# A dense–SiLU–dense forward and backward kernel: GpSimd clears the semaphores before its wait for the last store, waits in the barrier's release, and takes the last count off behind it

## The chip, the cores and the metric

The kernel runs on one core of one Trainium2 chip. The metric is the device's time for one execution in microseconds (us), on that core; lower is better. The "span" of a run is the part of it from the program's first instruction to the end of its last one. Every run told here was in the fast state (one-look runs are marked "unknown" for lack of a second run to compare), at a granted TensorE clock of 0.999 to 1.000, and every kernel gave the right result.

## The reference, cut to what matters

```
x: (1, 2048, 640)   w1: (640, 1536)   w2: (1536, 640)   grad_out: (1, 2048, 640)   all bf16
h   = silu(x @ w1)
out = h @ w2
returns out and the gradients of x, w1 and w2 for grad_out
```

The last output to be finished is the gradient of w1. Nothing of the mathematics is touched by the change. What matters is how the program ends.

## The kernel before: its end

The gradient of w1 is stored in pieces; the last piece is split into one of 384 and one of 128 columns, so that the very last store is small:

```python
# ... (inside the loop over the last block of w1's gradient)
for k, (lo, hi) in enumerate(((0, FC - P), (FC - P, FC))):
    gp = ps_h.tile([P, FC], FP32, name="hp")
    # ... 16 matmuls into gp[:, lo:hi]
    g1 = s1pool.tile([P, FC], dt_in, name="g1")
    # ... copied by ScalarE (k == 0) or VectorE (k == 1)
    store = nc.sync.dma_start(out=gw1_v[:, dt_, fc * FC + lo:fc * FC + hi], in_=g1[:, lo:hi])
    last_stores.append(store.ins.name)
last_stores_end_on_pool(nc, last_stores)
```

After that the framework appends a closing block: SyncE waits for everything that is still open, all engines meet in a first barrier, GpSimd clears the program's semaphores (here numbers 99 to 110), and all engines meet in a second barrier. In a barrier each of the four other engines raises a "gather" semaphore (96), GpSimd waits for four of these, then raises a "release" semaphore (97) by four, and each engine takes one off as its receipt. `last_stores_end_on_pool` edits this block when the program is finalized:

```python
def last_stores_end_on_pool(nc, names):
    def move(nc):
        # ... lanes: the semaphores of the two last stores; waits: SyncE's list of open waits
        late = [w for lane in reversed(lanes) for w in waits if w.id == lane]
        waits = [w for w in waits if w.id not in lanes]           # SyncE no longer waits for them
        # ...
        drain, gather, release, reset, clear, drain2, gather2, release2 = pool
        # ... gather2, reset, clear, drain2 are taken out
        reset = copy.replace(reset, sync_info=mybir.SyncInfo(on_wait=late, on_update=[]))
        for i in (drain2, clear, reset, gather2):                 # put back in the order
            end.insert(to, i)                                     # gather2, reset, clear, drain2

    nc.at_finalize(move)
```

So GpSimd's closing sequence before is: gather, release | gather2, wait for store 107, drain that waits for store 108 (`reset`), clear 99 to 110, drain, release2. Numbers 107 and 108 are the semaphores of the two last stores; a store has landed when its semaphore has got 16 more counts. After this the runtime's own closing code follows, which is no part of the program.

## Time and profile before

| kernel before | |
|---|---|
| time, first three runs | 320.31 us median (319.86 to 320.56) |
| span of the profiled run | 318.5 us |
| TensorE busy | 315.5 us, 99% |
| granted TensorE clock | 1.000 |
| last store: issue to its 16th count | 1.443 us |
| its 16th count to the end of the span | 0.423 us |
| end of the span to the last count of the runtime's barriers | 1.908 us |

The page of the profile of the kernel before: its span, busy time by engine (microseconds, share of the span, number of records), and the chain of work that ended last, by engine.

```profile
span 318.5 us, 3634 instructions
PE 315.5 (99%) x1529; PEld 147.5 (46%) x1529; DVE 103.0 (32%) x183; ACT 77.4 (24%) x139; POOL 0.7 (0%) x6
...
PE 98%; DMA 1%; DVE 0%; issue 0%; DVEq 0%; SPq 0%
```

TensorE is the bottleneck from 2.8 us to 316.2 us, and everything else hides behind it. A change that touches neither matmuls nor loads can act on the start or on the end alone.

The timeline of the kernel before from 311.5 us on (start, duration, engine, line, operation), its last lines. "SPq" is SyncE's queue: two issues, merged.

```profile
315.38 0.49 ACT L431 ACTIVATE g<-hp 128x384 bf16<-128x384 f32 x1 [5.46 <-PE hp L422]
315.89 1.08 SPq L434 DMA_DIRECT2D out_dram<-g  x2
316.32 0.29 DVE L433 CAST g<-hp 128x128 bf16<-128x128 f32 x1 [2.80 <-PE hp L422]
```

The timeline shows the engines' work and the DMA issues only, so nothing after 316.97 us is in it, though the span lasts to 318.51. The last 1.5 us are semaphore and drain instructions of the sequencers. The view of one source line counts them; here that of the line to which the closing block is put, GpSimd alone, from 310 us (count, durations in ns as minimum/median/maximum, first and last start):

```profile
L481 POOLq EVENT_SEMAPHORE  x5: 17/17/17, 317.4 to 318.4; - x5
L481 POOLq DRAIN  x2: 34/56/78, 318.1 to 318.3; - x2
L481 POOLq EVENT_SEMAPHORE_RANGE_CLEAR  x1: 96/96/96, 318.2 to 318.2; - x1
```

Both drains and the clear start at or after 318.1 us, behind the last store. The trace's own records have them one by one (start in us from the span's start, duration in ns, what; "16th count" is the last of the sixteen updates of a store's semaphore):

```
316.644  332  SyncE   issue of the last store (128x128)
317.512       16th count of semaphore 107 (the store before the last)
317.714   17  GpSimd  gather2
317.810   17  GpSimd  wait for 107
318.087       16th count of semaphore 108 (the last store)
318.111   78  GpSimd  drain, waits for 108
318.217   96  GpSimd  range clear 99..110
318.342   34  GpSimd  drain
318.406   17  GpSimd  release2
318.459   51  TensorE receipt; ends at 318.510, the end of the span
318.743, .777, .984, 319.028, .052, .150, .189, .223, .270    semaphore 2 (the runtime's barrier)
319.169 to 319.837   the runtime clears all semaphores
320.061 to 320.418   semaphore 2 again, nine times
```

Two things are needed to read this. The Trainium skill, "Perfetto Trace Analysis", section "Sequencer-only Instruction (DRAIN, etc)", says that a record begins when all awaited semaphores are satisfied, not when the wait begins. The trace agrees: the drain that waits for 108 has its start 24 ns after the 16th count, although GpSimd was free 0.28 us earlier. So the cost of a sequence has to be read from the spacing of starts, and the wait is the gap. And "Runtime: NRT & Kernel Launch", section "Semaphores 0–2 are reserved", names semaphore 2 as that of the runtime's barrier; its section "The ~15µs preamble/postamble breakdown" puts a barrier and a clearing of semaphores after the kernel. The records above agree, with the nine counts from 318.743 to 319.270. Below, each of these nine is called a step of the runtime's barrier; the third is at 318.984. That each step belongs to one engine is a reading.

### The profile page before, as it was taken

How to read it: one execution, taken by the hardware profiler on the slowest of the kernel's cores; microseconds unless marked ns; L12 is line 12 of the kernel's file. 1: busy time of each engine (PE TensorE's matmuls, PEld its weight loads, DVE VectorE, ACT ScalarE, POOL GpSimd, SP SyncE). 2: the span in 40 equal slices, each digit the busy share in tenths (PEclk: the TensorE clock that was granted, in tenths of full speed). 3: DMA queues.
4: the chain of work that ended last, by engine and by line, in shares of the span. 5: the costliest groups of instructions: out<-in, count | busy, mean ns of one | idle time of the engine just before them, and what ended most of it. 6: DMA issues, size and time to landing. Idle time of an engine off the chain costs nothing.

```text
span 318.5 us, 3634 instructions
## 1 busy us (share of the span) xinstructions
PE 315.5 (99%) x1529; PEld 147.5 (46%) x1529; DVE 103.0 (32%) x183; ACT 77.4 (24%) x139; POOL 0.7 (0%) x6
## 2 busy tenths in 40 slices
PE   9999999999999999999999999999999999999997
PEld 6644444444444444444444444444444444444444
DVE  1387641477410187710147741000000100001001
ACT  3492000644201354411064520110100001001010
POOL 0000000000000000000000000000000000000000
PEclk9999999999999999999999999999999999999999
DMA  9999999999799874492635079919999999996011
GB/s 242 332 182 190 238 283 239 350 291 311 233 229 320 199 228 113 145 302 83 166 105 145 0 259 268 216 24 299 254 243 261 251 209 341 245 264 217 33 35 49
DMA packets 147264, 66.85 MB, mean 210 GB/s; under 512 B 113328, under 2 KB 146736, under 8 KB 147248
## 3 DMA queue, kind: packets, MB, share of 16 engines
q1 hardware_dynamic: 146960, 66.33, 82.6%
q10 hardware_dynamic: 288, 0.30, 0.3%
q8 instruction: 12, 0.20, 0.2%
q14 instruction: 4, 0.03, 0.0%
HBM read 9.18 MB, written 28.97 MB: 120 GB/s over the span
## 4 chain that ended last, share of the span: by engine, by line
PE 98%; DMA 1%; DVE 0%; issue 0%; DVEq 0%; SPq 0%
PE hp L302 33%; PE hp L286 16%; PE hp L391 16%; PE hp L442 15%; PE hp L223 14%; PE hp L254 3%; PE hp L422 1%; DMA x_nat<-in_x_dram 1%; PE tp L212 1%; DVE g L433 0%; DVEq L433 0%; SPq L470 0%
## 5 line engine op out<-in xcount | busy, mean ns | idle before, releaser
L286 PE MATMUL hp<-goT,w2T 128*128 128x512 bf16 x240 | 56.9, 379 | 0.0
L302 PE MATMUL hp<-aT,w_nat 128*128 128x512 bf16 x240 | 52.5, 379 | 0.0
L302 PE MATMUL hp<-ghT,w1T 128*128 128x512 bf16 x240 | 52.5, 379 | 0.0
L391 PE MATMUL hp<-a_blk,go_nat 128*128 128x512 bf16 x240 | 52.0, 379 | 0.0
L442 PE MATMUL hp<-gh_blk,x_nat 128*128 128x512 bf16 x224 | 48.5, 379 | 0.0
L223 PE MATMUL hp<-xT,w_nat 128*128 128x512 bf16 x200 | 48.2, 379 | 0.0
L310 ACT ACTIVATE oT<-hp 128x512 bf16<-128x512 f32 x24 | 14.4, 598 | 104.3 <-PE hp L302 104.3
L232 ACT ACTIVATE aT<-hp 128x512 bf16<-128x512 f32 x48 | 28.5, 614 | 37.4 <-PE hp L223 30.4
L302 PEld LDWEIGHTS <-w1T 128*128 128x128 bf16 x240 | 23.5, 98 | 28.3
L302 PEld LDWEIGHTS <-w_nat 128*128 128x128 bf16 x240 | 23.5, 98 | 28.3 <-DMA w_nat<-in_w_dram 0.2
L391 PEld LDWEIGHTS <-go_nat 128*128 128x128 bf16 x240 | 23.5, 98 | 28.3
L286 PEld LDWEIGHTS <-w2T 128*128 128x128 bf16 x240 | 23.5, 98 | 28.3
L293 DVE SCALAR_TENSOR_TENSOR ghT<-ghT,hp 128x512 bf16<-128x512 bf16 x48 | 32.5, 682 | 7.0 <-PE hp L286 7.0
L442 PEld LDWEIGHTS <-x_nat 128*128 128x128 bf16 x224 | 21.9, 98 | 26.4
L312 DVE CAST oT<-hp 128x512 bf16<-128x512 f32 x16 | 11.0, 691 | 70.6 <-PE hp L302 70.6
L239 DVE SCALAR_TENSOR_TENSOR ghT<-aT,v 128x512 bf16<-128x512 bf16 x48 | 32.6, 686 | 0.3
L223 PEld LDWEIGHTS <-w_nat 128*128 128x128 bf16 x200 | 19.5, 98 | 23.4
L238 DVE TENSOR_SCALAR v<-t 128x512 bf16<-128x512 f32 x48 | 20.1, 425 | 28.1 <-ACT t L236 28.1
L236 ACT ACTIVATE t<-hp 128x512 f32<-128x512 f32 x44 | 26.5, 620 | 0.0
L453 DVE CAST g<-hp 128x512 bf16<-128x512 f32 x7 | 4.8, 692 | 47.0 <-PE hp L442 28.0
L401 DVE CAST g2T<-hp 128x512 bf16<-128x512 f32 x7 | 4.8, 692 | 46.1 <-PE hp L391 46.1
L399 ACT ACTIVATE g2T<-hp 128x512 bf16<-128x512 f32 x8 | 4.8, 597 | 47.0 <-PE hp L391 47.0
(24 smaller groups left out, 43.7 us busy)
## 6 DMA issues: line engine op xcount, KB each, us to landing
aT_scr<-aT SPq DMA_DIRECT2D x4, 1536.0 KB, 6.2
ghT_scr<-ghT SPq DMA_DIRECT2D x4, 1536.0 KB, 8.0
out_dram<-o_sb SPq DMA_DIRECT2D x8, 640.0 KB, 3.5
oT_scr<-oT SPq DMA_DIRECT2D x4, 640.0 KB, 4.3
go_nat<-in_grad_out_dram SPq DMA_DIRECT2D x4, 640.0 KB, 6.5
gxT_scr<-oT SPq DMA_DIRECT2D x4, 640.0 KB, 5.7
w_nat<-in_w_dram SPq DMA_DIRECT2D x1, 1920.0 KB, 12.5
x_nat<-in_x_dram SPq DMA_DIRECT2D x3, 640.0 KB, 7.0
```

The source lines that it names most:

```text
L223: nc.tensor.matmul(hp[:], lhsT=w1_nat[:, dt_, ft * P:(ft + 1) * P], rhs=xT[:, dt_, :], start=(dt_ == 0), stop=(dt_ == DT - 1),)
L232: nc.scalar.activation(aT[:, ft, :], hp[:], ACT.Silu)
L236: nc.scalar.activation(t[:], hp[:], ACT.Tanh, scale=0.5)
L238: nc.vector.tensor_scalar(out=v[:], in0=t[:], scalar1=-0.5, scalar2=0.5, op0=ALU.mult, op1=ALU.add)
L239: nc.vector.scalar_tensor_tensor(out=ghT[:, ft, :], in0=aT[:, ft, :], scalar=1.0, in1=v[:], op0=ALU.subtract, op1=ALU.mult)
L286: nc.tensor.matmul(gp[:], lhsT=w2T[:, dt_, ft * P:(ft + 1) * P], rhs=goT[:, dt_, :], start=(dt_ == 0), stop=(dt_ == DT - 1),)
L293: nc.vector.scalar_tensor_tensor(out=ghT[:, ft, :], in0=ghT[:, ft, :], scalar=1.0, in1=gp[:], op0=ALU.add, op1=ALU.mult)
L302: nc.tensor.matmul(op_[:], lhsT=w_all[:, ft, dt_ * P:(dt_ + 1) * P], rhs=rhs_all[:, ft, :], start=(ft == 0), stop=(ft == FT - 1),)
L310: nc.scalar.activation(oT[:, dt_, :], op_[:], ACT.Copy)
L312: nc.vector.tensor_copy(out=oT[:, dt_, :], in_=op_[:])
L391: nc.tensor.matmul(gp[:], lhsT=go_nat[:, st, dt_ * P:(dt_ + 1) * P], rhs=a_blk[:, st, :], start=(st == 0), stop=(st == ST - 1),)
L442: nc.tensor.matmul(gp[:], lhsT=x_nat[:, st, dt_ * P:(dt_ + 1) * P], rhs=gh_blk[:, st, :], start=(st == 0), stop=(st == ST - 1),)
```

## The change

The intent: 0.295 us of drains and clearing lie between the first instruction after the arrival of the last store (318.111) and the release (318.406). Do the clearing while the store is still in flight. The semaphore of the last store cannot be cleared then, so the cleared range is split around it, the release itself waits for the store, and one more instruction takes the 192 counts off afterwards.

```diff
@@ -52,21 +53,52 @@
         end = blocks[-1].instructions
         at = next(k for k, i in enumerate(end) if i.engine == mybir.EngineType.SP)
         waits = list(end[at].sync_info.on_wait)
-        late = [w for lane in reversed(lanes) for w in waits if w.id == lane]
+        late = [w for lane in lanes for w in waits if w.id == lane]
         assert len(late) == len(names) and not end[at].sync_info.on_update
         waits = [w for w in waits if w.id not in lanes]
         end[at] = copy.replace(end[at], sync_info=mybir.SyncInfo(on_wait=waits, on_update=[]))
+
         pool = [i for i in end if i.engine == mybir.EngineType.Pool]
         drain, gather, release, reset, clear, drain2, gather2, release2 = pool
         assert gather2.sync_info.on_wait and not release2.sync_info.on_wait
-        assert all(i.sync_info is None or not i.sync_info.on_wait for i in (reset, clear, drain2))
-        closing = {i.name for i in (reset, clear, drain2, gather2)}
+        assert all(i.sync_info is None for i in (reset, clear, drain2))
+        last = late[-1]
+        first, stop = reset.reset_range_start, reset.reset_range_stop
+        assert first <= last.id < stop and list(clear.instr[12:15]) == [1, first, stop - 1]
+        cleared = []
+        for lo, hi in ((first, last.id), (last.id + 1, stop)):
+            if lo < hi:
+                cleared.append(
+                    copy.replace(reset, name=nc.get_next_instruction_name(), reset_range_start=lo, reset_range_stop=hi)
+                )
+                cleared.append(
+                    copy.replace(
+                        clear,
+                        name=nc.get_next_instruction_name(),
+                        instr=clear.instr[:13] + (lo, hi - 1) + clear.instr[15:],
+                        ant_dict={**clear.ant_dict, "range_first": lo, "range_last": hi - 1},
+                    )
+                )
+        cleared[0] = copy.replace(cleared[0], sync_info=mybir.SyncInfo(on_wait=late[:-1], on_update=[]))
+        (total,) = gather2.sync_info.on_update
+        off = copy.replace(total, id=last.id, ant_name=last.ant_name, update_value=last.wait_value)
+        tail = [gather2, *cleared, drain2]
+        tail.append(
+            copy.replace(
+                release2, sync_info=mybir.SyncInfo(on_wait=[last], on_update=list(release2.sync_info.on_update))
+            )
+        )
+        tail.append(
+            copy.replace(
+                release2, name=nc.get_next_instruction_name(), sync_info=mybir.SyncInfo(on_wait=[], on_update=[off])
+            )
+        )
+        closing = {i.name for i in pool[3:]}
         to = next(k for k, i in enumerate(end) if i.name == reset.name)
         for k in reversed(range(len(end))):
             if end[k].name in closing:
                 del end[k]
-        reset = copy.replace(reset, sync_info=mybir.SyncInfo(on_wait=late, on_update=[]))
-        for i in (drain2, clear, reset, gather2):
+        for i in reversed(tail):
             end.insert(to, i)
 
     nc.at_finalize(move)
```

GpSimd's closing sequence after it: gather, release | gather2, drain that waits for 107, clear 99 to 107, drain, clear 109 to 110, drain, release2 that waits for 108, count-off of 108. No other engine's instructions differ.

## The prediction

> **What bounds the kernel now.** TensorE: the busy table gives PE 315.5 of 318.5 us (99%), the chain of waits PE 98%, at full granted clock (1.000). The change touches no matmul, transfer or buffer, only instructions after the last store is issued, so it can act on the last microsecond alone.
>
> **That microsecond, from the trace's records of sequencer instructions (us from the span's start).** SyncE issues the last store at 316.644. GpSimd collects the second barrier's arrivals at 317.714; its wait for the first of the two last stores starts at 317.810 and costs nothing (landed at 317.512). The last store's 16th count comes at 318.087. Only then GpSimd runs drain 318.111 (78 ns), range clear 318.217 (96 ns), drain 318.342 (34 ns), release 318.406. TensorE's receipt ends the span at 318.510. So 0.295 us (318.111 to 318.406) is serial between the store's arrival and the release: the most that the change can take off.
>
> **What the change does.** It moves that work ahead of the last wait, puts the wait on the release, and splits the clear in two (9 semaphores, then 2), each behind a drain. It adds a drain and a clear, drops a separate wait, and adds one instruction behind the release that subtracts the last count.
>
> **Costs.** By start-to-start spacing in the trace, a drain that doesn't wait takes 64 ns, one that waited 106, the 12-semaphore clear 125, a semaphore instruction 66 to 96. After 317.714 GpSimd starts its first drain at about 317.80, then 64 to 106 (drain), 120 (clear), 64 (drain), 105 (clear), 64 (drain): estimate of the release, 318.22 to 318.26. The store is there at 318.09. So the moved work, about 0.42 us, doesn't fit in the gap of 0.30 us before the store's arrival; the release becomes bound by GpSimd's own sequence, and the gain there is about 0.17 us (0.08 to 0.24), not 0.295.
>
> **What is given back.** The count-off stands after the release on GpSimd: +0.08 us (estimate from the 79 ns spacing of two of its semaphore instructions). The Trainium skill's page "Runtime: NRT & Kernel Launch", section "The ~15µs preamble/postamble breakdown", says that a barrier of all engines and a reset of the semaphores follow the kernel. The trace agrees: semaphore 2 is raised nine times from 318.743 to 319.270. Its third step comes 207 ns after its second, against 38 ns in the other barriers; I take the late third engine to be GpSimd (the order is a guess). If so, GpSimd ends the kernel's time and the 0.08 us is paid in full; if not, it is hidden.
>
> **Prediction.** The span falls by about 0.17 us (to 318.2 to 318.45), the time by about 0.1 us: 320.2 us. Runs of before spread from 319.86 to 320.56, so the range is 319.75 to 320.6. Faster by over 2%: 0.01; within 2%: 0.98; slower: 0.01.
>
> **What would show each step.** Right: matmul rows, clock and DMA unchanged; two clears on GpSimd between 317.8 and 318.25, at 105 to 125 ns each; the release over 0.05 us after the last store's 16th count; one more semaphore instruction 80 to 96 ns after it; the runtime barrier shifted earlier by less than the release. Wrong: the release within 30 ns of the 16th count (the clears fitted, gain near 0.3 us); or the barrier shifted as much as the release (count-off free).
>
> **What would make it wrong.** A last store that lands later than in this one profile and leaves the clears more room; a second drain or clear much dearer than the first; a barrier that waits for another engine than GpSimd; above all scatter between runs, larger than the effect.

## The result, and the profile after

| | before | after |
|---|---|---|
| time, median of 6 runs each | 320.16 us (319.55 to 320.56) | 320.07 us (319.55 to 320.62) |
| ratio after/before | | 1.000, 95% interval 0.9985 to 1.0016 |
| span of the profiled run | 318.51 us | 317.68 us |
| **from the issue of the last store:** | | |
| 16th count of the last store | +1.443 | +1.445 |
| release2 | +1.762 | +1.664 |
| GpSimd's last instruction starts | +1.762 | +1.742 |
| third step of the runtime's barrier | +2.340 | +2.320 |
| last count of the runtime's barriers | +3.774 | +3.755 |

A ratio is the mean time of one kernel's fast runs over that of the other's of the same rounds, so it isn't quite the ratio of the medians quoted. The time is the same to within its interval of 0.15%, some 0.5 us. All outputs are right.

The page of the kernel after, the same three lines:

```profile
span 317.7 us, 3608 instructions
PE 313.5 (99%) x1501; PEld 147.3 (46%) x1529; DVE 103.0 (32%) x183; ACT 77.4 (24%) x139; POOL 0.7 (0%) x6
...
PE 98%; DMA 1%; issue 1%; DVE 0%; DVEq 0%; SPq 0%
```

The span looks 0.83 us shorter, which would be a gain of 0.3%. It isn't one. (Nor has the kernel lost 28 matmuls: PE has 1501 records against 1529, but the weight loads are 1529 in both; a few matmul records are missing from this trace.) The chain that ended last shows where the span differs. Here are its pieces in the first 16 us (start, duration, what), of before:

```profile
0.08 2.73 DMA x_nat<-in_x_dram
...
2.85 1.78 PE tp L212 x15
4.64 9.39 PE hp L254 x80
```

and of after:

```profile
0.08 2.55 DMA x_nat<-in_x_dram
...
2.68 1.78 PE tp L244 x15
4.46 8.84 PE hp L286 x80
```

The first load of x landed 0.18 us sooner, and the first 80 matmuls, which begin while loads of w1 are still arriving, took 0.55 us less: 0.73 us in all, in code that the change doesn't touch. From the 43rd weight load (6.4 us) to the last (316.0 us) the two traces run in step, with an offset of 0.728 to 0.730 us in all but one of these 1487 loads. Only the remaining 0.098 us can belong to the change. It was the fastest of the six runs that was profiled: the spans of all six run from 317.7 to 318.8 us. Scatter of the start is what moves the time of this kernel from run to run, and it is several times the whole effect. So from here on landmarks are counted from the issue of the last store, where that scatter is gone.

GpSimd in the closing block of the kernel after, from 310 us (the same view of one source line; the block's line number has moved from 481 to 513):

```profile
L513 POOLq EVENT_SEMAPHORE  x5: 17/17/17, 316.6 to 317.7; - x5
L513 POOLq DRAIN  x3: 40/60/76, 317.1 to 317.5; - x3
L513 POOLq EVENT_SEMAPHORE_RANGE_CLEAR  x2: 45/68/92, 317.2 to 317.4; - x2
```

The two clears are there, of 92 and 45 ns, with a third drain. Record by record:

```
after the last store's issue, us (duration ns); spacing to the next start, ns
+1.095 (17)  gather2                    95
+1.190 (76)  drain, 107 has landed     105
+1.295 (92)  clear 99..107             121
+1.416 (60)  drain                      89
+1.445       16th count of the last store
+1.505 (45)  clear 109..110             75
+1.580 (40)  drain                      84
+1.664 (17)  release2, waits for 108    78
+1.742 (17)  count-off of 108
+1.768       TensorE's receipt ends, the end of the span
+2.001 +2.036 +2.320 +2.364 +2.387 ...  the runtime's barrier
```

When the store arrives, the second drain is still running. The release comes 0.219 us after the 16th count, where an instruction that was waiting for it would start about 0.02 us after. And of the 0.098 us that the release gained, the runtime's barrier kept 0.020: GpSimd's last instruction had moved by only 0.020 us, because of the count-off behind the release. From GpSimd's last instruction to the third step it is 0.578 us in both traces.

### The profile page after: what moved, and what is told of

Read it like the earlier page. It is cut to its first block, busy times and chain, and to the rows that moved or that the text cites. A ratio compares the mean times of both kernels' runs of the same rounds, so it can differ in the third digit from the quotient of the medians.

```text
span 317.7 us, 3608 instructions
## 1 busy us (share of the span) xinstructions
PE 313.5 (99%) x1501; PEld 147.3 (46%) x1529; DVE 103.0 (32%) x183; ACT 77.4 (24%) x139; POOL 0.7 (0%) x6
## 4 chain that ended last, share of the span: by engine, by line
PE 98%; DMA 1%; issue 1%; DVE 0%; DVEq 0%; SPq 0%
PE hp L334 32%; PE hp L318 16%; PE hp L423 16%; PE hp L474 15%; PE hp L255 13%; PE hp L286 3%; PE hp L454 1%; DMA x_nat<-in_x_dram 1%; PE tp L244 1%; DVE g L465 0%; DVEq L465 0%; SPq L502 0%
```

## The experiments

The theory: (a) the release is bound by GpSimd's own sequence of two clears and three drains and not by the store; (b) GpSimd is the third engine of the runtime's barrier and the last to arrive there, so everything behind the release on GpSimd is paid in full. The rivals: the small differences are scatter; the count-off is hidden because the runtime's barrier waits for another engine; the landing of the store bounds the end whoever waits for it.

All landmarks are from one profile of each kernel, in us after the issue of the last store. The last column is the time of that profiled run minus the moment of the issue in it; it follows the landmarks, which shows that the runtime's barriers are part of the measured time.

| kernel | release2 | GpSimd's last | 3rd step | last count | time minus issue |
|---|---|---|---|---|---|
| before | 1.762 | 1.762 | 2.340 | 3.774 | 3.65 |
| before_again | 1.764 | 1.764 | 2.342 | 3.775 | 3.64 |
| after | 1.664 | 1.742 | 2.320 | 3.755 | 3.64 |
| after_again | 1.633 | 1.711 | 2.290 | 3.720 | 3.60 |
| count_off_by_12 | 1.644 | 2.584 | 3.158 | 4.618 | 4.49 |
| count_off_by_12_on_sp | 1.634 | 1.634 | 2.207 | 3.863 | 3.74 |
| no_count_off | 1.638 | 1.638 | 2.217 | 3.674 | 3.55 |
| one_clear | 1.465 | 1.543 | 2.121 | 3.585 | 3.46 |
| no_clear | 1.463 | 1.541 | 2.119 | 3.551 | 3.42 |
| early_pool_waits | 1.554 | 1.632 | 2.205 | 3.637 | 3.51 |
| early_sp_waits | 1.440 | 1.440 | 2.013 | 3.446 | 3.31 |
| early_one_clear | 1.260 | 1.260 | 1.839 | 3.271 | 3.15 |

### Controls: the two kernels once more

No edit.

> The changed kernel once more, as a control for one profile's scatter. All landmarks are counted from the issue of the last store. In the first profiles: before has the last store's 16th count at +1.443, the release at +1.762, the third step of the runtime's barrier at +2.340 and its last count at +3.774 us; after has +1.445, +1.664, +2.320 and +3.755. My theory (the release is bound by GpSimd's own chain of two clears; the count-off behind it is paid in full): the same four landmarks within 0.03 us. Rival (the small differences between the two kernels are scatter of the landmarks): release and third step move by 0.05 us or more from the first profile of this kernel.

> The kernel before once more, as a control for the landmarks of one profile, counted from the issue of the last store. Theory: 16th count +1.44, release +1.76, third step of the runtime's barrier +2.34, each within 0.03 us, so that the changed kernel's two profiles (third step +2.32 and +2.29) are earlier by 0.02 to 0.05. Rival (the difference of the two kernels is scatter): third step at +2.31 or less.

Measured: after_again's release at +1.633 and third step at +2.290; before_again's release at +1.764 and third step at +2.342. In each profile of the changed kernel the time from gather2 to release2 is 0.569 us; the 0.031 us by which its two releases differ is that of gather2 (+1.095 and +1.064), which waits for TensorE's arrival at the second barrier. So the release gained 0.098 and 0.129 us over before, and the third step 0.020 and 0.050. after_again misses the 0.03 us that its expectation had allowed, by 0.001 us at the release and 0.005 us at the last count (+3.720 against +3.755), but stays short of the 0.05 us of its rival. The odd one is the first profile: in the nine profiles in which no clear stands ahead of it, gather2 comes at +1.064 to +1.076, but for the +1.095 there. One profile of a kernel repeats to about 0.03 us here. So the gain at the release is clear of the scatter; that at the third step is of the scatter's size, and its exact amount is not shown. The time: 320.14 us against 320.38 us of before, ratio 0.9999 (0.9984 to 1.0014), which can't resolve it.

### The count-off taken in twelve steps, on GpSimd

```diff
@@ -91,3 +91,6 @@
-        tail.append(
-            copy.replace(
-                release2, name=nc.get_next_instruction_name(), sync_info=mybir.SyncInfo(on_wait=[], on_update=[off])
+        part = copy.replace(off, update_value=16)
+        for _ in range(last.wait_value // 16):
+            tail.append(
+                copy.replace(
+                    release2, name=nc.get_next_instruction_name(), sync_info=mybir.SyncInfo(on_wait=[], on_update=[part])
+                )
@@ -95 +97,0 @@
-        )
```

> GpSimd takes the last store's count of 192 off in 12 steps of 16 instead of one. Theory (GpSimd is the last engine into the runtime's barrier, so each instruction behind its release is paid): third step of the barrier at about +3.18 us after the last store's issue, 11 times 0.078 = 0.86 us later than in the changed kernel, and the time 0.86 us longer (ratio to before near 1.0025). Rival (the runtime's barrier waits for another engine, the count-off is hidden): third step and time unchanged, or up by far less than 0.86 us.

Measured: third step at +3.158, the count-offs 78 ns apart, and 0.574 us from GpSimd's last instruction to the third step. The first and second steps stayed at +1.982 and +2.016: two other engines had arrived and waited for the third. The time was 321.11 us against 320.38 us, ratio 1.0031 (1.0015 to 1.0048). The extra instructions are paid in full; the third engine is GpSimd, and it is the one that the runtime waits for. The prediction's guess of the order is thereby shown for this step.

### The same twelve steps, on SyncE

```diff
@@ -91,5 +90,0 @@
-        tail.append(
-            copy.replace(
-                release2, name=nc.get_next_instruction_name(), sync_info=mybir.SyncInfo(on_wait=[], on_update=[off])
-            )
-        )
@@ -102,0 +98,11 @@
+        sp_last = [i for i in end if i.engine == mybir.EngineType.SP][-1]
+        at_sp = next(k for k, i in enumerate(end) if i.name == sp_last.name)
+        for _ in range(12):
+            end.insert(
+                at_sp + 1,
+                copy.replace(
+                    sp_last,
+                    name=nc.get_next_instruction_name(),
+                    sync_info=mybir.SyncInfo(on_wait=[], on_update=[copy.replace(off, update_value=16)]),
+                ),
+            )
```

> The same 12 steps of 16, but on SyncE, behind its receipt of the release; none on GpSimd. Theory: GpSimd's third step comes 0.078 us earlier than in the changed kernel (about +2.24 us after the last store's issue), and SyncE, which stands at the fifth step, has some 0.3 to 0.5 us of slack against 12 times about 0.067 = 0.80 us, so the barrier ends 0.2 to 0.5 us later than in the changed kernel, not 0.8. Rival (an instruction at the end costs the same on every engine): +0.7 to 0.8 us.

Measured: the third step at +2.207. SyncE's last instruction ended at +2.425 and the fifth step came at +2.554, so with twelve steps SyncE, the fifth engine, does become the last. The barriers ended at +3.863, 0.11 to 0.14 us later than in the changed kernel, where twelve steps on GpSimd had cost 0.86 to 0.90. My expectation of 0.2 to 0.5 us was too high: SyncE's count-offs are 57 to 74 ns apart, 60 in the mean, and not 67, and it needs only 0.129 us from its last instruction to its step. The plainest comparison is with the next run, which has no count-off at all and ends at +3.674: the twelve steps cost 0.189 us on SyncE and 0.944 us on GpSimd. The same work costs far less on an engine that isn't awaited. The time, 320.02 us against 320.38, ratio 0.9992 (0.9977 to 1.0008), can't resolve the 0.09 us by which the landmarks put it behind before.

### No count-off

```diff
@@ -91,5 +90,0 @@
-        tail.append(
-            copy.replace(
-                release2, name=nc.get_next_instruction_name(), sync_info=mybir.SyncInfo(on_wait=[], on_update=[off])
-            )
-        )
```

> The changed kernel without the count-off; the last store's semaphore is left at 192 for the runtime to clear. Theory: release unchanged (about +1.66 us after the last store's issue), third step of the barrier 0.078 us earlier (about +2.24), so the whole is 0.10 us shorter than before where the changed kernel was 0.02. Time minus span about 1.79 us as before, against 1.86 for the changed kernel. Rival (the count-off is hidden): third step stays at +2.32 us and time minus span at 1.86.

Measured: release at +1.638, third step at +2.217, that is 0.073 to 0.103 us earlier than with it. The time minus the span, which can be read in every run, not only in the profiled one (spans are listed to 0.1 us), averages 1.79 us over 7 runs of before, 1.87 over 6 and 1.85 over 4 runs of the changed kernel, and 1.79 over 4 runs without the count-off. So the count-off is paid in all runs. The median time, 320.47 us, and ratio 1.0015 (0.998 to 1.005) say nothing: one of the four runs took 322.25 us, with a span of 320.5, which is scatter ahead of the end.

### One clear

```diff
@@ -69 +69 @@
-        for lo, hi in ((first, last.id), (last.id + 1, stop)):
+        for lo, hi in ((first, last.id),):
```

> The changed kernel without the second drain and clear (two semaphores are left for the runtime to clear); the count-off stays. Landmarks from the issue of the last store; the changed kernel has 0.569 us from GpSimd's second collection (+1.07) to its release (+1.64), of which the second drain and clear take 0.164. Theory: the release comes 0.164 us earlier, at about +1.475, some 0.03 us after the last store's 16th count (+1.44), and the third step of the runtime's barrier at about +2.13 instead of +2.29. Rival (the release waits for the store and the clears are hidden behind it): no change.

Measured: release at +1.465, 0.025 us after the 16th count (+1.440), and the third step at +2.121. The release moved by 0.168 to 0.199 us, the 0.164 us of the second drain and clear and the scatter of gather2. GpSimd's own sequence now ends at almost the moment at which the store lands, so this run alone can't say which of the two binds; the next one can. The time, 320.31 us against 320.2, ratio 0.9998 (0.9984 to 1.0012), doesn't show the 0.19 us by which the last count comes sooner than in before, though its interval doesn't exclude it.

### No clear

```diff
@@ -85 +85,4 @@
-        tail = [gather2, *cleared, drain2]
+        arrived = copy.replace(
+            release2, name=nc.get_next_instruction_name(), sync_info=mybir.SyncInfo(on_wait=late[:-1], on_update=[])
+        )
+        tail = [gather2, arrived, drain2]
```

> The changed kernel without either clear and their drains; one semaphore instruction waits for the first of the last two stores, one drain stays, the count-off stays. GpSimd's own chain would be through at about +1.33 us after the last store's issue. Theory: the release now waits for the store and comes 0.024 us after its 16th count, at +1.46 us: only about 0.02 us earlier than with one clear, though 0.23 us more work is gone; third step of the barrier about +2.12. Rival (the release is bound by work on GpSimd alone, or the barrier by another engine): the release at +1.33, or a third step that doesn't follow.

Measured: release at +1.463, third step at +2.119. The clear and a drain gone, a wait added, and only 0.002 us gained, though GpSimd was at its last drain by +1.221: the floor is the store's arrival plus 0.024 us. Together with the run before, this shows (a): of the 0.569 us from gather2 to the release, what goes beyond the store's arrival is paid, and the rest isn't. The time was 319.36 us, ratio 0.998 (0.9966 to 0.9994), that is 0.2 to 1.1 us less than before. The landmarks explain 0.22 us, at the edge of that; the last store was issued at 315.95 us in its profile, against 316.64 and 316.70 in the two of before, so a lucky start can have made up the rest.

Both kernels leave semaphores for the runtime to clear, whose clearing stands in every trace (319.169 to 319.837 us in that of before; a record of one semaphore or two is missing in some). They are experiments, not proposals.

### Both clears early, the wait on SyncE

GpSimd idles 0.25 us between its first release and gather2. The clears of semaphores that nobody waits for any more can go there. SyncE then waits for the two stores and takes their counts off, behind its last receipt.

```diff
@@ -69 +69 @@
-        for lo, hi in ((first, last.id), (last.id + 1, stop)):
+        for lo, hi in ((first, late[0].id), (last.id + 1, stop)):
@@ -82 +81,0 @@
-        cleared[0] = copy.replace(cleared[0], sync_info=mybir.SyncInfo(on_wait=late[:-1], on_update=[]))
@@ -84,12 +83,3 @@
-        off = copy.replace(total, id=last.id, ant_name=last.ant_name, update_value=last.wait_value)
-        tail = [gather2, *cleared, drain2]
-        tail.append(
-            copy.replace(
-                release2, sync_info=mybir.SyncInfo(on_wait=[last], on_update=list(release2.sync_info.on_update))
-            )
-        )
-        tail.append(
-            copy.replace(
-                release2, name=nc.get_next_instruction_name(), sync_info=mybir.SyncInfo(on_wait=[], on_update=[off])
-            )
-        )
+        offs = [copy.replace(total, id=x.id, ant_name=x.ant_name, update_value=x.wait_value) for x in late]
+        assert late[0].id + 1 == last.id
+        tail = [*cleared, drain2, gather2, release2]
@@ -102,0 +93,11 @@
+        sp_last = [i for i in end if i.engine == mybir.EngineType.SP][-1]
+        at_sp = next(k for k, i in enumerate(end) if i.name == sp_last.name)
+        for x, off in reversed(list(zip(late, offs))):
+            end.insert(
+                at_sp + 1,
+                copy.replace(
+                    sp_last,
+                    name=nc.get_next_instruction_name(),
+                    sync_info=mybir.SyncInfo(on_wait=[x], on_update=[off]),
+                ),
+            )
```

> Both clears stand between GpSimd's first release and its second collection, where it idles 0.25 us; SyncE waits for the two last stores behind its receipt of the second release and takes their counts off there; GpSimd waits for no store. Theory: two clears cost 0.45 us there, so the second collection comes 0.28 us later (about +1.36), the second release at +1.44, about 0.2 us earlier than in the changed kernel, and the third step of the runtime's barrier 0.58 us later, at about +2.02 (before +2.34, changed +2.29 to +2.32); the time about 0.3 us shorter than before. SyncE's part is hidden. Rival (the landing of the store bounds the end whoever waits for it): third step no earlier than in the kernel without the count-off, +2.2.

Measured: gather2 at +1.362, release at +1.440, third step at +2.013. GpSimd's way of 0.573 us to the runtime's barrier now runs beside the store's landing (+1.446) and not behind it. This alone hardly refutes the rival that the landing bounds the third step whoever waits. The expectation set the bar at +2.2, but the kernel without the count-off was itself bound by its clears. A release bound by the landing, with no count-off behind it, would put the third step at about +2.04 (an estimate: no_clear's +2.119 less the 0.078 us of its count-off), only 0.03 us later than measured. The last run decides it. SyncE ended at +1.659, and the fifth step came 0.067 us after the third as in before (0.068), so its part is hidden. The time: 319.87 us against 320.2, ratio 0.9991 (0.9977 to 1.0004).

### Both clears early, the waits left on GpSimd

This keeps the early clears and puts both waits and count-offs back on GpSimd.

```diff
@@ -69 +69 @@
-        for lo, hi in ((first, last.id), (last.id + 1, stop)):
+        for lo, hi in ((first, late[0].id), (last.id + 1, stop)):
@@ -82 +81,0 @@
-        cleared[0] = copy.replace(cleared[0], sync_info=mybir.SyncInfo(on_wait=late[:-1], on_update=[]))
@@ -85 +84,8 @@
-        tail = [gather2, *cleared, drain2]
+        assert late[0].id + 1 == last.id
+        off0 = copy.replace(total, id=late[0].id, ant_name=late[0].ant_name, update_value=late[0].wait_value)
+        tail = [*cleared, drain2, gather2]
+        tail.append(
+            copy.replace(
+                release2, name=nc.get_next_instruction_name(), sync_info=mybir.SyncInfo(on_wait=[late[0]], on_update=[off0])
+            )
+        )
```

> Both clears early as in the run before, but GpSimd keeps both waits and both count-offs: it separates moving the clears from moving the wait to SyncE. Theory: second collection at +1.36, the first store's wait and count-off cost 0.16 us more, so the release at about +1.52, over 0.05 us after the store's 24 ns, the count-off at +1.60 and the third step at about +2.18: 0.17 us later than with the waits on SyncE (+2.013) and about 0.11 to 0.14 earlier than the changed kernel. Rival (all the gain came from the early clears): third step at +2.02.

Measured, in one look: release at +1.554, third step at +2.205, so 0.192 us later than with the waits on SyncE, and 0.085 to 0.115 earlier than in the changed kernel. Release and third step came 0.03 us later than expected. Moving the clears accounts for the 0.085 to 0.115 us, net of a count-off of 107 that the changed kernel doesn't have; what SyncE takes over is worth the 0.192 us. That is work and not waiting: both stores had landed (+0.871 and +1.435) well before the instruction that waits for each started (+1.458 and +1.554). From gather2 to GpSimd's last instruction there are three steps here, of 96, 96 and 78 ns, where the run before has one of 78.

### One early clear, four count-offs on SyncE

```diff
@@ -69 +69 @@
-        for lo, hi in ((first, last.id), (last.id + 1, stop)):
+        for lo, hi in ((first, late[0].id),):
@@ -82 +81,0 @@
-        cleared[0] = copy.replace(cleared[0], sync_info=mybir.SyncInfo(on_wait=late[:-1], on_update=[]))
@@ -84,12 +83,5 @@
-        off = copy.replace(total, id=last.id, ant_name=last.ant_name, update_value=last.wait_value)
-        tail = [gather2, *cleared, drain2]
-        tail.append(
-            copy.replace(
-                release2, sync_info=mybir.SyncInfo(on_wait=[last], on_update=list(release2.sync_info.on_update))
-            )
-        )
-        tail.append(
-            copy.replace(
-                release2, name=nc.get_next_instruction_name(), sync_info=mybir.SyncInfo(on_wait=[], on_update=[off])
-            )
-        )
+        over = [x for x in waits if x.id > last.id]
+        assert sorted(x.id for x in over) == list(range(last.id + 1, stop))
+        late = over + late
+        offs = [copy.replace(total, id=x.id, ant_name=x.ant_name, update_value=x.wait_value) for x in late]
+        tail = [*cleared, drain2, gather2, release2]
@@ -102,0 +95,11 @@
+        sp_last = [i for i in end if i.engine == mybir.EngineType.SP][-1]
+        at_sp = next(k for k, i in enumerate(end) if i.name == sp_last.name)
+        for x, off in reversed(list(zip(late, offs))):
+            end.insert(
+                at_sp + 1,
+                copy.replace(
+                    sp_last,
+                    name=nc.get_next_instruction_name(),
+                    sync_info=mybir.SyncInfo(on_wait=[x], on_update=[off]),
+                ),
+            )
```

> As the one before, but GpSimd clears only the eight lower semaphores; SyncE takes the four upper counts off at its end, each with its own wait. Theory: second collection at about +1.19, release +1.27, third step about +1.85, so 0.45 to 0.5 us off before, unless SyncE (about 0.26 us behind the release and behind the landing at +1.44) becomes the last; its fifth step should then come by +1.9. Time about 319.8 against 320.3 of before. Rival (landing bounds the end): third step at +2.0 or later.

GpSimd in the closing block of this kernel, the same view as above:

```profile
L516 POOLq EVENT_SEMAPHORE  x4: 17/17/17, 317.6 to 318.1; - x4
L516 POOLq DRAIN  x2: 34/53/72, 317.7 to 317.9; - x2
L516 POOLq EVENT_SEMAPHORE_RANGE_CLEAR  x1: 77/77/77, 317.8 to 317.8; - x1
```

One clear and two drains are left, and GpSimd is done at 318.1 us; the last store was issued at 316.842 in this run, so its 16th count came at 318.273, after GpSimd's last instruction. Measured: gather2 at +1.182, release at +1.260, third step at +1.839, fifth at +1.905, last count at +3.271, which is 0.50 us earlier than before. The third step lies 0.20 us below the +2.04 that a landing-bound release would give, so the landing doesn't bound the end here. The time: 319.58 us (319.24 to 319.99, 5 runs) against 320.2 us (9 runs), ratio 0.9981 (0.9968 to 0.9993). By the landmarks this version beats both kernels, before by 0.50 us and the changed one by 0.45 to 0.48. The runs' 0.6 us (0.2 to 1.0) over before agree, but wouldn't carry it alone: no_clear had the same ratio with 0.22 us in its landmarks. It was not timed in the same rounds as the changed kernel. Its price: the program's own barrier no longer stands behind the last store, and only SyncE's wait, which the runtime's barrier joins, holds the end.

## Why the prediction was right

- **The time.** Predicted 320.2 us (319.75 to 320.6), within 2%; measured 320.07 us, ratio 1.000. The gain of 0.1 us that the prediction named is 0.02 to 0.05 us by the landmarks; the times can't resolve either. The range took in the three runs of before, so a forecast of no change would have passed as well: that the number was right says nothing for the mechanism, which rests on the landmarks.
- **The clears don't fit before the store's arrival.** Right: the release came 0.219 us after the 16th count, 0.198 in after_again (over 0.05 had been predicted), and one_clear and no_clear show that it moves with GpSimd's work until 0.024 us after the 16th count, and no further.
- **The gain at the release.** Predicted about 0.17 us (0.08 to 0.24); measured 0.098 and 0.129. The mechanism held, and a term was mis-sized: the way from gather2 to the release was taken as 0.51 to 0.55 us (317.714 to 318.22 or 318.26) and measured 0.569, and in the first profile gather2 itself came 0.025 us later than in before. The drains were spaced 105, 89 and 84 ns where I had used 64 for those that don't wait. The second clear was cheaper, 75 against 105 ns. "At 105 to 125 ns each" was right for the first clear (121) and wrong for the second. An early clear's drain that waits for nothing was also spaced 101 ns, so the 106 of before weren't the price of waiting.
- **The count-off is paid in full.** Right: 78 ns behind the release, predicted 0.08 us (the sign given, 80 to 96 ns, was missed by 2 ns); the twelvefold dose and its removal show it, and with it the guess that the late third engine is GpSimd.
- **The span.** Predicted 318.2 to 318.45 us, measured 317.68. Not the change: 0.729 us of the 0.83 came in the first 6.4 us. The prediction's warning that scatter exceeds the effect was right, but it drew the span's range too narrow for it.
- **Left open.** Why GpSimd needs 0.57 us from its last instruction to its step of the runtime's barrier, where SyncE needs at most 0.13, no record shows. Nor is it shown why the first loads of one run land sooner than those of another.

## What to carry to other kernels

Work moved ahead of a wait is free only up to the time that the wait leaves, so measure that gap and add up the moved sequence by start-to-start spacing before you split it into more instructions. At the end of a program find the engine for which the next barrier waits: an instruction behind the release on that engine is paid in full, while here another engine with slack took it, and even the wait itself, at no cost in the barrier. When an effect is smaller than the scatter of the start, compare landmarks counted from the last event that both kernels share, and confirm a cheap cost by multiplying it.

## What the Trainium skill lacked or had wrong

- "Runtime: NRT & Kernel Launch" doesn't say in which order the engines step through the runtime's barrier, nor that they need different times to get there. Here GpSimd takes the third step, 0.573 to 0.579 us after the start of its last instruction wherever it is the last to arrive, and SyncE took the fifth 0.129 us after the end of its last instruction when it was last.
- The same page, "The ~15µs preamble/postamble breakdown", gives about 1.5 us each for the closing barrier and for the reset of semaphores. In the trace of before the barrier's last count came 0.864 us after the program's last release, and the clearing of all semaphores took 0.67 us (319.169 to 319.837). Whether the page counts the same stretches isn't said there. Its figure of about 355 ns for the steps across the engines, given for the barrier ahead of the kernel, agrees: 0.357 us in the second closing barrier (320.061 to 320.418).
- No page has the cost of a semaphore range clear on GpSimd. The records show clears of 96, 92, 77 and 45 ns for 12, 9, 8 and 2 semaphores, each between drains whose next instruction, where it had nothing to wait for, starts 64 to 106 ns after them.
